# Soft-capped attention with a maxout layer: moving the q/k transposes of 36 of 48 head pairs from TensorE to the DMA crossbar, and reordering the weights' loads

## The chip, the cores and the metric

One core of one Trainium2 chip. The metric is the device time of one execution in microseconds (us). The kernel before was run four times beside the changed one, 437.27 to 440.6 us, median 439.74 (438.88 for the three runs known at the time of the prediction). Where a ratio is given, it is the mean time of one kernel's fast runs over the mean time of the other's fast runs of the same rounds, so it isn't quite the ratio of the medians that are quoted; the interval behind it is a 95% interval.

The views of the profile name the engines so: PE is TensorE's matmuls and PEld its weight loads, DVE is VectorE, ACT is ScalarE, POOL is GpSimd and SP is SyncE, which here only issues DMA transfers. PSUM is the memory that takes the matmuls' results. "Crossbar call" stands for one transposing DMA (DMA_TRANSPOSE in the profile).

## The reference

```python
# q, k, v: (8 batches, 12 heads, 448, 64) f32; cap = 30
scores = q @ k.T / sqrt(64)
scores = cap * tanh(scores / cap)
attn   = softmax(scores)                 # over 448 keys
x      = (attn @ v), heads side by side  # (3584, 768)
g      = maximum(x @ w1, x @ w2)         # w1, w2: (768, 1024)
out    = g @ w_out                       # (3584, 768)
```

The kernel uses max(h1, h2) = relu(h1 - h2) + h2: it keeps `wd = w1 - w2` and the product `wm = w2 @ w_out`, so that `out = relu(x @ wd) @ w_out + x @ wm`.

## The kernel before

Work goes by pairs of heads: 48 pairs, six per batch, loaded in 16 groups of three. A pair's q and k come in natural order, are cast to bf16 by POOL, and are turned by eight TensorE transposes into the unused half of a scores bank in PSUM; DVE copies them out:

```python
def transposes(i, ps):                     # ps = spare[i-1], a scores bank's unused half
    for t, o in ((kf, 0), (qf, Q0)):
        for j in range(4):
            nc.tensor.transpose(ps[:, o + j*P : o + (j+1)*P], t[g % 2][:, n, j, :], ident)
    qkT[i] = att.tile([P, 8 * P], bf16, name="qkT", bufs=3)
    nc.vector.tensor_copy(qkT[i], ps)
```

Then come scores, tanh and exp (ACT), attention times V into the one `pv` buffer, and DVE's copy `u` of it (5 buffers). Sums of the softmax leave `u` by small DMAs; every second pair they are inverted, sent to DRAM and read back spread over the partitions; POOL multiplies with them. All of these DMAs, and all loads of q, k and v, are issued by SP, in program order:

```python
def invert(g):                             # g: group of two pairs
    nc.vector.reciprocal(t, sums[g])
    nc.sync.dma_start(out=d, in_=t)                                   # rec_d <- rec_s
    for h in range(2):
        nc.sync.dma_start(out=rb[...], in_=flat[...].to_broadcast(...))  # rec_b <- rec_d
```

The weights come during the first nine pairs, issued by POOL, and are prepared as follows; `premultiply` and the two products of a finished batch are "filler" that is doled out to TensorE between the attention steps (`F(n)` gives n matmuls) and that writes into two PSUM buffers `mm`:

```python
def cast_w12(c):
    nc.gpsimd.tensor_copy(w2b, w2c)
    nc.vector.tensor_sub(wd_sb[:, c, :], w1c, w2c)
...
for i in range(N):                         # cut to the order of the parts
    pv_main(i); ex(i+1, 0, 4); pv_left(i); qk(i+1, 2); pv_out(i)
    F(8)
    qk(i+1, 3); ex(i+1, 4, 7)
    # casts and loads of coming groups; cast_w12, load_w12 in the first pairs
    F(6)
    transposes(i+2, spare[i+1])
    F(6)
    # even i: invert(last group);  odd i: normalize(POOL, last group)
    qk(i+2, 0); qk(i+2, 1)
    F(5)
```

## Time and profile before

I cut the 437.9 us of the profiled execution at two marks: the start of attention times V of pair 12 and of pair 47. The page of the kernel before gives the totals; the table of stretches (columns: stretch, its length, busy time of PE, PEld, DVE, ACT and POOL with their instructions, granted clock, DMA share, GB/s) gives the stages:

```profile
0.00:127.79 127.79, 88.21 (x523) 40.35 (x524) 55.70 (x90) 80.52 (x81) 66.35 (x94) 0.85 0.65 183
127.79:385.20 257.41, 252.92 (x1661) 126.75 (x1658) 118.30 (x177) 212.37 (x210) 135.80 (x166) 0.99 0.50 142
385.20:437.90 52.70, 42.31 (x236) 23.39 (x234) 16.48 (x28) 0.00 (x0) 4.51 (x4) 0.94 0.20 71
```

| stage of the kernel before | us | reading |
|---|---|---|
| front, to pair 12 | 127.8 | PE busy 69%, clock 0.85: waits |
| long stage, pairs 12 to 46 | 257.4 | PE busy 98%: TensorE is the bound |
| tail | 52.7 | 10 us of PE idle |

The timeline of the kernel before (start, length, engine, line, operation, out<-in, and in brackets the idle time ahead of it) has this in the long stage:

```profile
220.86 0.48 DVE L262 RECIPROCAL rec_s<-sums 32x56 f32<-32x56 f32 x1
221.59 0.54 SPq L264 DMA_DIRECT2D rec_d<-rec_s  x1
228.33 4.71 POOL L284 TENSOR_TENSOR xT<-u,rec_b 64x448 bf16<-64x448 f32 x4 [4.09 <-DMA rec_b<-rec_d]
```

In this kernel no reciprocal of the 24 waited more than 1.0 us for SP.

### The profile page before, as it was taken

How to read it: one execution, taken by the hardware profiler on the slowest of the kernel's cores; microseconds unless marked ns; L12 is line 12 of the kernel's file. 1: busy time of each engine (PE TensorE's matmuls, PEld its weight loads, DVE VectorE, ACT ScalarE, POOL GpSimd, SP SyncE). 2: the span in 40 equal slices, each digit the busy share in tenths (PEclk: the TensorE clock that was granted, in tenths of full speed). 3: DMA queues.
4: the chain of work that ended last, by engine and by line, in shares of the span. 5: the costliest groups of instructions: out<-in, count | busy, mean ns of one | idle time of the engine just before them, and what ended most of it. 6: DMA issues, size and time to landing. Idle time of an engine off the chain costs nothing.

```text
span 437.9 us, 6546 instructions
## 1 busy us (share of the span) xinstructions
PE 383.4 (88%) x2416; PEld 190.5 (44%) x2416; DVE 190.5 (44%) x294; ACT 292.9 (67%) x289; POOL 206.7 (47%) x263
## 2 busy tenths in 40 slices
PE   3570777779999999999998999999979999994996
PEld 1220333334455455544553555455434555452553
DVE  5322444545543553445345534554335344523422
ACT  4782564558798879887987798879858898810000
POOL 3381786751736573555554736563655424440000
PEclk9966786889999999999999999999989999996999
DMA  5999666632445646575655456646553212122012
GB/s 146 274 258 255 209 183 235 195 105 75 129 136 166 178 114 177 141 223 136 178 150 156 111 156 190 198 125 172 164 158 107 80 63 91 44 80 78 37 57 89
DMA packets 74016, 63.70 MB, mean 145 GB/s; under 512 B 24832, under 2 KB 68864, under 8 KB 73984
## 3 DMA queue, kind: packets, MB, share of 16 engines
q1 hardware_dynamic: 71168, 55.41, 44.5%
q0 software_dynamic: 2816, 7.87, 5.9%
q8 instruction: 19, 0.31, 0.3%
q14 instruction: 13, 0.11, 0.1%
HBM read 53.48 MB, written 11.18 MB: 148 GB/s over the span
## 4 chain that ended last, share of the span: by engine, by line
PE 71%; DMA 10%; POOL 8%; SPq 4%; DVE 3%; issue 3%; DVEq 0%; POOLq 0%
PE mm L297 17%; PE mm L312 15%; PE mm L309 11%; PE pv L232 10%; PE s L212 6%; POOL xT L284 4%; PE s L196 4%; DMA w_in<-in_moe_w_dram 4%; PE mm L177 4%; PE pv L241 3%; DMA rec_b<-rec_d 2%; SPq L111 2%; DMA rec_d<-rec_s 2%; PE s L215 1%; SPq L100 1%
## 5 line engine op out<-in xcount | busy, mean ns | idle before, releaser
L213 ACT ACTIVATE tanh<-s 128x896 bf16<-128x896 f32 x144 | 126.0, 909 | 77.9 <-PE s L212 77.8
L284 POOL TENSOR_TENSOR xT<-u,rec_b 64x448 bf16<-64x448 f32 x92 | 104.2, 1133 | 141.7 <-DMA rec_b<-rec_d 137.0
L220 ACT ACTIVATE expo<-tanh 128x1792 bf16<-128x1792 bf16 x96 | 145.0, 1510 | 3.0
L245 DVE COPY u<-pv 128x896 f32<-128x896 f32 x48 | 52.4, 1091 | 92.4 <-PE pv L241 85.8
L312 PE MATMUL mm<-wo_sb,gT 128*128 128x384 bf16 x448 | 91.7, 330 | 0.0
L297 PE MATMUL mm<-xT,wd_sb 128*128 128x448 bf16 x384 | 84.5, 357 | 4.1 <-POOL xT L284 4.1
L309 PE MATMUL mm<-wm_sb,xT 128*128 128x384 bf16 x336 | 70.6, 330 | 6.5 <-DVE osb L316 6.5
L232 PE MATMUL pv<-expo,vp 128*128 128x448 bf16 x288 | 66.8, 371 | 0.0
L212 PE MATMUL s<-qkT 64*128 64x448 bf16 x288 | 46.6, 377 | 15.0 <-DVE qkT L198 14.4
L312 PEld LDWEIGHTS <-gT 128*128 128x128 bf16 x448 | 41.9, 99 | 35.2 <-issue 11.4
L198 DVE COPY qkT<-s 128x1024 bf16<-128x1024 bf16 x47 | 32.5, 691 | 52.9 <-PE s L196 36.4
L297 PEld LDWEIGHTS <-wd_sb 128*128 128x128 bf16 x384 | 35.1, 99 | 43.1 <-issue 16.6
L301 DVE TENSOR_SCALAR gT<-mm 128x448 bf16<-128x448 f32 x64 | 39.7, 621 | 27.9 <-PE mm L297 27.2
L316 DVE COPY osb<-mm 128x384 f32<-128x384 f32 x56 | 30.8, 552 | 38.7 <-PE mm L312 38.4
L309 PEld LDWEIGHTS <-xT 128*128 128x128 bf16 x336 | 31.4, 99 | 32.9 <-issue 15.1
L232 PEld LDWEIGHTS <-vp 128*128 128x128 bf16 x288 | 28.7, 101 | 29.1 <-issue 6.1
L177 PE MATMUL mm<-wo_sb,w2T 128*128 128x384 bf16 x96 | 23.8, 392 | 13.6 <-DVE w2T L172 13.6
L217 ACT ACTIVATE tanh<-s 128x448 bf16<-128x448 f32 x48 | 26.0, 542 | 9.9 <-PE s L215 8.2
L196 PE MATMUL s<-ident,kf 128*128 128x128 bf16 x188 | 19.4, 230 | 6.3 <-ACT tanh L217 6.3
L131 POOL CAST kf<-km 128x1152 bf16<-128x1152 f32 x15 | 17.2, 1143 | 15.6 <-DMA km<-in_k_dram 12.7
L212 PEld LDWEIGHTS <-qkT 64*128 64x128 bf16 x288 | 10.6, 96 | 32.0 <-DVE qkT L198 28.5
L196 PEld LDWEIGHTS <-kf 128*128 128x128 bf16 x192 | 15.7, 103 | 19.1 <-issue 8.1
(50 smaller groups left out, 228.6 us busy)
## 6 DMA issues: line engine op xcount, KB each, us to landing
rec_b<-rec_d SPq DMA_DIRECT2D x48, 224.0 KB
out_dram<-osb SPq DMA_DIRECT2D x24, 384.0 KB
km<-in_k_dram SPq DMA_DIRECT2D x15, 576.0 KB
qm<-in_q_dram SPq DMA_DIRECT2D x15, 576.0 KB
vm<-in_v_dram SPq DMA_DIRECT2D x15, 576.0 KB
w_in<-in_moe_w_dram POOLq DMA_DIRECT2D x12, 512.0 KB, 5.0
sums<-u SPq DMA_DIRECT2D x96, 1.8 KB
wo_sb<-in_moe_w_out_dram POOLq DMA_DIRECT2D x4, 384.0 KB, 7.9
```

What stands on the lines that cost most here:

```text
L177: nc.tensor.matmul(ps[:, : DM // 2], w2T[:, f * P : (f + 1) * P], wo_sb[:, f, hs], start=(f == 0), stop=(f == FC - 1),)
L196: nc.tensor.transpose(ps[:, o + j * P : o + (j + 1) * P], t[g % 2][:, n, j, :], ident)
L212: nc.tensor.matmul(s[:, h, :S], t[r, j * P : (j + 1) * P], qTn[r, :])
L213: nc.scalar.activation(tanh[i][:, 2 * j : 2 * j + 2, :], s[:, :, :S], AF.Tanh, scale=scale / cap)
L220: nc.scalar.activation(expo[i][:, c0:c1, :], tanh[i][:, c0:c1, :], AF.Exp, scale=float(cap))
L232: nc.tensor.matmul(ps[:, h, :S], vp[g % 2][:, n, h, j, :], e[:, 2 * j + h, :], start=(j == 0), stop=False)
L245: nc.vector.tensor_copy(u, pvt[i][:, :, :S])
L284: eng.tensor_mul(xT[b // 2][r, hp, cs], U[i][r, h, :], rec[g][r, n, :])
L297: nc.tensor.matmul(ps[:, :S], wd_sb[:, c, f * P : (f + 1) * P], x[:, c, cs], start=(c == 0), stop=(c == KC - 1))
L301: nc.vector.tensor_relu(g[:, f, cs], ps[:, :S])
L309: nc.tensor.matmul(ps[:, : DM // 2], x[:, c, ts], wm_sb[:, c, hs], start=(c == 0), stop=False)
L312: nc.tensor.matmul(ps[:, : DM // 2], g[:, f, ts], wo_sb[:, f, hs], start=False, stop=(f == FC - 1))
```

## The change

The intent: take transposes off TensorE where it is the bound. Pairs 0 to 11 are still transposed by TensorE, now into the filler's `mm` buffers; from pair 12 on, one DMA-transpose call on SP turns the q and k of three pairs at once. w2 arrives as bf16 through a casting DMA, w1 is loaded by SP, the subtraction moves to the end of a pair, the filler of batch 0 is queued behind the premultiplication, and half of the last normalization goes to POOL. Cut to its core:

```diff
-    def cast_w12(c):
-        nc.gpsimd.tensor_copy(w2b, w2c)
-        nc.vector.tensor_sub(wd_sb[:, c, :], w1c, w2c)
+    def load_w2(c):
+        nc.gpsimd.dma_start(out=w2b[:, c, :], in_=moe_w2[c * P : (c + 1) * P, :])     # casts
+    def load_w1(c):
+        nc.sync.dma_start(out=w1_in[c], in_=moe_w1[c * P : (c + 1) * P, :])
+    def subtract(c):
+        nc.vector.tensor_sub(wd_sb[:, c, :], w1_in[c], w2b[:, c, :])
...
-    def transposes(i, ps):
+    def transposes(i):
+        ps = mm_psum.tile([P, 512], f32, name="mm").bitcast(bf16)
...
+    def cross(g):
+        nc.sync.dma_start_transpose(
+            out=qkT_of(g).rearrange("p n j c -> p (n j) c"), in_=kqf[g % 2].rearrange("p n j c -> p (n j c)")
+        )
...
+    NT = 4
+    for g in range(2, NL):                 # loads and casts of k, q, v: cut
+        if g >= NT:
+            at(3 * g - 4, cross, g)
+    for c in range(KC):
+        at(c // 3, load_w2, c)
+        at(2 + c, load_w1, c)
...
-        if i + 2 < N:
-            transposes(i + 2, spare[i + 1])
+        if i + 2 < NT * L:
+            transposes(i + 2)
...
+        if 3 <= i < 3 + KC:
+            subtract(i - 3)
```

More of the change, by code (lines that the diff above doesn't have):

```diff
@@ L64 @@
     vl = [const.tile([P, L, P], bf16, name=f"vl{i}") for i in range(2)]
-    kf = [const.tile([P, L, 4, P], bf16, name=f"kf{i}") for i in range(2)]
-    qf = [const.tile([P, L, 4, P], bf16, name=f"qf{i}") for i in range(2)]
+    kqf = [const.tile([P, L, 8, P], bf16, name=f"kqf{i}") for i in range(2)]
+    kf = [t[:, :, 0:4, :] for t in kqf]
+    qf = [t[:, :, 4:8, :] for t in kqf]
     ident = const.tile([P, P], bf16, name="ident")
@@ L143, in cast @@
                 eng.tensor_copy(t[r, n0:n1, 3, r], l[r, n0:n1, :])
-    w_in = {}
+    w1_in = {}
+    w2b = (
+        xpool.tile([P, FC, 2 * S], bf16, name="gT", bufs=1)
+        .rearrange("p f s -> p (f s)")[:, : KC * DF]
+        .rearrange("p (c n) -> p c n", c=KC)
+    )
     def load_wo(f):
@@ L151, in load_wo @@
         )
-    def load_w12(c):
-        w_in[c] = [stage.tile([P, DF], f32, name=n) for n in ("w1_in", "w2_in")]
-        for src, dst in zip((moe_w1, moe_w2), w_in[c]):
-            nc.gpsimd.dma_start(out=dst, in_=src[c * P : (c + 1) * P, :])
-    def cast_w12(c):
-        w1c, w2c = w_in[c]
-        w2b = stage.tile([P, DF], bf16, name="w2b", bufs=1)
-        nc.gpsimd.tensor_copy(w2b, w2c)
-        nc.vector.tensor_sub(wd_sb[:, c, :], w1c, w2c)
-        w_in[c] = w2b
+    def load_w2(c):
+        nc.gpsimd.dma_start(out=w2b[:, c, :], in_=moe_w2[c * P : (c + 1) * P, :])
+    def load_w1(c):
+        w1_in[c] = stage.tile([P, DF], f32, name="w1_in")
+        nc.sync.dma_start(out=w1_in[c], in_=moe_w1[c * P : (c + 1) * P, :])
+    def subtract(c):
+        nc.vector.tensor_sub(wd_sb[:, c, :], w1_in[c], w2b[:, c, :])
     def premultiply(c):
@@ L168, in premultiply @@
         for f in range(FC):
-            nc.tensor.transpose(ps[:, f * P : (f + 1) * P], w_in[c][:, f * P : (f + 1) * P], ident)
+            nc.tensor.transpose(ps[:, f * P : (f + 1) * P], w2b[:, c, f * P : (f + 1) * P], ident)
             yield
@@ L188, with qkT_of @@
     qkT = {}
-    spare = {}
-    def transposes(i, ps):
-        g, n = divmod(i, L)
-        for t, o in ((kf, 0), (qf, Q0)):
-            for j in range(4):
-                nc.tensor.transpose(ps[:, o + j * P : o + (j + 1) * P], t[g % 2][:, n, j, :], ident)
-        qkT[i] = att.tile([P, 8 * P], bf16, name="qkT", bufs=3)
-        nc.vector.tensor_copy(qkT[i], ps)
+    def qkT_of(g):
+        if g not in qkT:
+            qkT[g] = stage.tile([P, L, 8, P], bf16, name="qkT")
+        return qkT[g]
+    def transposes(i):
+        g, n = divmod(i, L)
+        ps = mm_psum.tile([P, 512], f32, name="mm").bitcast(bf16)
+        for j in range(8):
+            nc.tensor.transpose(ps[:, j * P : (j + 1) * P], kqf[g % 2][:, n, j, :], ident)
+        nc.vector.tensor_copy(qkT_of(g)[:, n, :, :].rearrange("p j c -> p (j c)"), ps)
+    def cross(g):
+        nc.sync.dma_start_transpose(
+            out=qkT_of(g).rearrange("p n j c -> p (n j) c"), in_=kqf[g % 2].rearrange("p n j c -> p (n j c)")
+        )
     def qk(i, j):
-        t = qkT[i]
+        g, n = divmod(i, L)
+        t = qkT[g][:, n, :, :].rearrange("p j c -> p (j c)")
         o = Q0 + 64 * (i // NP % 2)
@@ L215, in qk @@
             nc.tensor.matmul(s[:, 0, :S], t[:, 3 * P : 4 * P], qTn)
-            spare[i] = s[:, 1, :].bitcast(bf16)
             nc.scalar.activation(tanh[i][:, 6, :], s[:, 0, :S], AF.Tanh, scale=scale / cap)
@@ L273, with normalize @@
     xT = {}
-    def normalize(eng, g):
+    def normalize(g, eng_a=nc.gpsimd):
         for n in range(G):
@@ L283, in normalize @@
                 r = slice(64 * h, 64 * h + 64)
-                eng.tensor_mul(xT[b // 2][r, hp, cs], U[i][r, h, :], rec[g][r, n, :])
+                (nc.gpsimd, eng_a)[1 - h].tensor_mul(xT[b // 2][r, hp, cs], U[i][r, h, :], rec[g][r, n, :])
     gT = {}
@@ L337, with at @@
     NL = N // L
+    NT = 4
+    todo = [[] for _ in range(N)]
+    def at(i, f, *a):
+        todo[i].append((f, a))
+    for g in range(2, NL):
+        e = 0 if g < NT else 2
+        at(3 * g - 6 - e, load, g, "k")
+        at(3 * g - 5 - e, load, g, "q")
+        at(3 * g - 4, load, g, "v")
+        at(3 * g - (5 if e else 4), cast, nc.gpsimd, g, "k")
+        at(3 * g - (5 if e else 3), cast, nc.gpsimd, g, "q")
+        at(3 * g - 2, cast, nc.gpsimd, g, "v")
+        if g >= NT:
+            at(3 * g - 4, cross, g)
+    at(1, cast, nc.gpsimd, 1, "v")
+    for c in range(KC):
+        at(c // 3, load_w2, c)
+        at(2 + c, load_w1, c)
+    MS = 4
     fill_const(nc.vector, 0)
@@ L345 @@
     for what in "kq":
-        load(2, what)
-    for what in "kq":
         cast(nc.vector, 0, what, 0, 1)
-    transposes(0, mm_psum.tile([P, 512], f32, name="mm").bitcast(bf16))
+    transposes(0)
     cast(nc.vector, 0, "v", 0, 1)
@@ L361 @@
         cast(nc.gpsimd, 1, what)
-    transposes(1, spare[0])
+    for f in range(0, FC, 2):
+        load_wo(f)
+    transposes(1)
     qk(1, 0)
@@ L367 @@
         b, hp = divmod(i, NP)
-        l, ln = divmod(i, L)
         g, n = divmod(i, G)
@@ L376 @@
         pv_out(i)
-        if 3 <= i < 3 + KC:
-            fill_q.append(premultiply(i - 3))
-        if hp == 2 and b > 0:
+        if MS <= i < MS + KC:
+            fill_q.append(premultiply(i - MS))
+        if i == MS + KC - 1:
+            fill_q.append(moe(0))
+        if hp == 2 and b > 1:
             fill_q.append(moe(b - 1))
@@ L384 @@
             ex(i + 1, 4, 7)
-        for m, what, lead in ((0, "v", 1), (1, "k", 2), (1, "q", 2)):
-            if ln == m and l + lead < NL:
-                cast(nc.gpsimd, l + lead, what)
-        for m, what, lead in ((0, "v", 2), (1, "k", 3), (2, "q", 3)):
-            if ln == m and l + lead < NL:
-                load(l + lead, what)
-        if i < 2:
-            load_wo(4 * i)
-            load_wo(4 * i + 2)
-        if 2 <= i < 2 + KC:
-            cast_w12(i - 2)
-        if 1 <= i < 1 + KC:
-            load_w12(i - 1)
-        F(6)
-        if i + 2 < N:
-            transposes(i + 2, spare[i + 1])
+        for f, a in todo[i]:
+            f(*a)
+        F(6)
+        if i + 2 < NT * L:
+            transposes(i + 2)
         F(6)
@@ L404 @@
         if i >= G + 1 and n == 1:
-            normalize(nc.gpsimd, g - 1)
+            normalize(g - 1)
         if i + 2 < N:
@@ L409 @@
         F(5)
+        if 3 <= i < 3 + KC:
+            subtract(i - 3)
+    F(16)
     invert(N // G - 1)
-    normalize(nc.vector, N // G - 1)
+    F(24)
     fill_q.append(moe(B - 1))
+    normalize(N // G - 1, nc.vector)
     F(10 ** 9)
```

## The prediction

> **What bounds the kernel now.** I read the busy table and the slices first, then a table of stretches, then the order of work in one steady period, then the two places where the table shows holes.
>
> ```profile
> PE 383.4 (88%) x2416; PEld 190.5 (44%) x2416; DVE 190.5 (44%) x294; ACT 292.9 (67%) x289; POOL 206.7 (47%) x263
> PE 71%; DMA 10%; POOL 8%; SPq 4%; DVE 3%; issue 3%; DVEq 0%; POOLq 0%
> ```
>
> The busy table and the chain that ended last: TensorE holds 71% of the chain, but 29% is something else, so the span has to be cut by stage. Table of stretches (columns: stretch, length, busy time of PE, PEld, DVE, ACT, POOL, clock, DMA share, GB/s):
>
> ```profile
> 0.00:35.00 35.00, 18.40 (x92) 6.59 (x92) 13.37 (x33) 24.39 (x25) 16.25 (x34) 0.90 0.92 226
> 35.00:45.00 10.00, 0.64 (x7) 0.13 (x4) 2.22 (x3) 0.82 (x1) 2.37 (x2) 0.54 0.81 230
> 45.00:62.00 17.00, 12.55 (x76) 5.67 (x73) 7.85 (x9) 12.19 (x12) 14.42 (x18) 0.80 0.67 210
> 62.00:107.00 45.00, 35.83 (x223) 17.63 (x221) 21.25 (x29) 26.34 (x27) 24.96 (x32) 0.84 0.52 162
> 127.00:385.00 258.00, 253.51 (x1664) 127.12 (x1663) 118.10 (x177) 213.16 (x210) 136.26 (x166) 0.99 0.50 142
> 385.00:438.00 53.00, 42.51 (x238) 23.49 (x235) 16.68 (x28) 0.00 (x0) 4.51 (x4) 0.94 0.20 70
> ```
>
> Three regimes: a front until 107 us with a dead hole at 35 to 45 us and low clocks; a long stage from 127 us in which PE is 98% busy at clock 0.99; a tail with 10 us of PE idle.
>
> One period of the long stage, timeline, PE (start, length):
>
> ```profile
> 219.23 0.49 PE L312 MATMUL mm<-wo_sb,gT 128*128 128x384 bf16 x2
> 219.55 0.39 PE L196 MATMUL s<-ident,kf 128*128 128x128 bf16 x4
> 219.78 0.39 PE L196 MATMUL s<-ident,qf 128*128 128x128 bf16 x4
> 220.00 1.14 PE L312 MATMUL mm<-wo_sb,gT 128*128 128x384 bf16 x6
> ```
>
> The eight transposes of a pair hold PE from 219.55 to 220.00: 0.45 us, 56 ns each, not the 222 to 231 ns that one record lasts (they overlap).
>
> The hole at 35 to 45 us, timeline, DVE:
>
> ```profile
> 42.60 1.22 DVE L162 TENSOR_TENSOR wd_sb<-w_in 128x1024 bf16<-128x1024 f32 x1 [8.68 <-DMA w_in<-in_moe_w_dram]
> 43.74 0.68 DVE L198 COPY qkT<-s 128x1024 bf16<-128x1024 bf16 x1
> ```
>
> The subtraction w1-w2 stands ahead of the copy of the transposes in DVE's queue and waits 8.7 us for the weights; the copy, and with it the next scores, wait behind it. Before that, ACT is the bound, with one wait per pair (timeline, ACT):
>
> ```profile
> 22.99 1.73 ACT L213 ACTIVATE tanh<-s 128x896 bf16<-128x896 f32 x2 [0.75 <-PE s L212]
> 29.77 1.73 ACT L213 ACTIVATE tanh<-s 128x896 bf16<-128x896 f32 x2 [0.74 <-PE s L212]
> ```
>
> Period 6.8 us, of which ACT works 6.05. The wait is there because the transposes are written in the spare half of a scores bank and so start only after the last tanh. The tail, timeline, DVE, then PE:
>
> ```profile
> 397.26 1.89 DVE L284 TENSOR_TENSOR xT<-u,rec_b 64x448 bf16<-64x448 f32 x3 [0.17 <-DMA rec_b<-rec_d]
> 399.18 1.02 DVE L316 COPY osb<-mm 128x384 f32<-128x384 f32 x2
> ```
>
> ```profile
> 399.79 2.08 PE L309 MATMUL mm<-wm_sb,xT 128*128 128x384 bf16 x6 [6.55 <-DVE osb L316]
> 401.66 2.76 PE L312 MATMUL mm<-wo_sb,gT 128*128 128x384 bf16 x8
> ```
>
> The last normalization stands on DVE ahead of evictions that PE needs, and waits for the reciprocals' round trip; PE loses 6.55 us, then runs 14 matmuls at half speed.
>
> **What the Trainium skill says.** "TensorE: Matmul & The Clock Gate", Part 4: PE-mode transpose, gives about 275 ns for a transpose in a kernel. The trace has 222 to 231 ns as length but 56 ns as spacing, and the spacing decides. The same page, Part 1: The HAM clock gate, says that an idle window of some 3.4 us halves the clock; the trace agrees (0.54 in the hole; the six matmuls at 399.79 took 2.08 us, those at 390.80 1.14), so a removed hole pays more than its length. "DMA: Bandwidth & Descriptors", Latency and other measured facts, gives 261 GB/s for a DMA transpose in one kernel, 350 to 400 when contiguous. Nothing in this trace measures it. The same page, Issuing engines are not separate DMA queues: transfers of SP and POOL run on the same 16 DMA engines. So moving w1 to SP buys order and not bandwidth; the trace's share of 0.92 in the first 35 us, with both queues in use, is in line with that.
>
> **The change part by part.**
>
> *Transposes.* 36 of the 48 pairs lose 8 transposes: 36 x 0.45 = 16.2 us of PE, 15.3 of them in the 34 periods between pair 12's attention-times-V (127.8 us) and pair 47's (385.2). Also 36 DVE copies of 691 ns = 25 us; DVE is 46% busy there, so these are worth nothing by themselves. Added: 12 crossbar calls on SP, each 128 x 3072 bf16 = 0.79 MB. At the page's 261 GB/s an estimate of 3 us each, one per three pairs (about 20 us). Each is issued some two and a half periods before its first use, about 16 us. The DMA share in the long stage would go from 0.50 to about 0.65. I take it as hidden.
>
> *Transposes of the first 12 pairs in the other PSUM pool.* They no longer wait for the last tanh: the 0.75 us wait goes, period 6.05 us in the pairs without filler.
>
> *Weights.* w2 comes as bf16 by a casting DMA (6 POOL casts of 1.55 us = 9.3 us go); the subtraction moves to the end of the period, behind the copies that the scores need; the premultiplication starts one pair later. Front, from pair to pair (starts of attention-times-V): pairs 0 to 3 took 45.3-16.4 = 28.9 us; 3 x 6.05 = 18.2, and I leave 3 us for weights that land late = 21.2. Pair 3 to 4: 9.8 becomes 6.05. Pairs 4 to 10: 58.1 us, with 2.7 us waits of PE for the w2T copy (which sits behind the subtraction) and half clock after each; the one old period whose w2T copy had no subtraction before it took 7.4 us, so 6 x 7.4 = 44.4. Pairs 10 to 12: 14.6 becomes 14.5 (0.9 less for transposes, more of the 448-column filler). Pair 12 then starts at 16.4+21.2+6.05+44.4+14.5 = 102.5 us in place of 127.8: 25 us gained.
>
> *Long stage.* 257.4 us less 15.3. Three periods hold waits for a late normalization, because the filler had run dry when the next batch's first product was started: 0.7, 1.4 and 4.3 us over the stall-free 7.68, together 6.3. By my count of filler steps (25 per pair offered, 24 per premultiplication, 132 or 160 per batch) the later start keeps 15 to 41 steps in stock at each batch's turn, so those go; 1.2 us come back, because slots that ran empty are filled. 257.4-15.3-6.3+1.2 = 237 us.
>
> *Tail.* 52.7 us from pair 47. The stock left then is 57 steps, with the 25 of the last period 82, each 0.1625 us = 13.3 us, enough to cover the reciprocal chain (normalization ended 14 us after pair 47 started). Half of the last normalization goes to POOL, and it stands after the evictions. The last batch, 48 x 0.189 + 112 x 0.1625 = 27.3 us, then starts at +14.8 in place of +21.4, and 3.9 us of output follow: 46 us.
>
> Sum: 102.5+237+46 = 385.5 us of span. I add 4 us for waits that I can't place and 1 us between span and measured time: **390 us**, 11% less.
>
> **Rivals.**
> 1. *The crossbar call is slow or clogs SP's queue.* Adding up the SP rows of the timeline from 147 to 390 us gives 134 us of issuing, 55%. If one call holds SP or the DMA rings for 10 us, SP comes to near 100%, sums and reciprocals queue behind, U's five buffers fill, and PE waits for attention results. Against: the lead of 16 us and one call per three pairs. For: the chain from sums to normalized xT is already tight (DVE waited 6.6 us for POOL to free U). Then the long stage gains nothing or loses: 410 to 450 us.
> 2. *The front is bound by DMA and not by order.* Loads of five groups and all weights are still needed by the same pair, and DMA ran at 226 to 230 GB/s at a share of 0.8 to 0.9 until 45 us. Then the hole moves to the premultiplication or the subtraction, and the front gains some 12 us: about 403 us.
> 3. *ACT takes over in the long stage.* A stall-free period goes from 7.0 to 7.7 down to 6.6 to 7.2, and ACT needs 6.05. PE stays the bound, but the margin of 0.5 us means that a small delay of scores is no longer free: 392 to 396 us.
>
> **Range and chances.** My sum has three large independent terms: 25 us in front (could be 12), 20 in the long stage (could be 0 with rival 1, 22 at best), 7 in the tail (4 to 8). A part of the front is lost with a chance of about one in four, a slow crossbar with one in eight. Range for 8 in 10: 377 to 408 us. The change is slower only if the crossbar truly bounds: faster by over 2% 0.91, within 2% 0.05, slower 0.04.
>
> **What would show it.** Right: no DVE copy of qkT after pair 11; PE period 6.6 us without transposes in the out-product stretches; no hole near 35 us and pair 12 near 102 us; no PE gap over 1 us near pair 38 or between pair 47 and the last batch; PE still 95% busy from pair 12 on. Wrong: PE or its weight loads waiting for the crossbar's DMA; SP waiting long for POOL's casts in front of a crossbar call; DVE's copy of U waiting for POOL; DVE's subtraction waiting for w1 or w2 past 40 us.

## The result, and the profile after

The changed kernel took 424.96 us (median of four, 423.34 to 425.88) beside 439.74 before: ratio 0.967 [0.962, 0.972], so 3.3% faster and not 11%. It is faster, but 424.96 lies well outside the predicted range.

The busy table and the chain that ended last, of the changed kernel:

```profile
PE 365.7 (86%) x2128; PEld 172.8 (41%) x2128; DVE 163.8 (39%) x256; ACT 292.3 (69%) x289; POOL 197.0 (46%) x253
PE 50%; DMA 21%; SPq 9%; POOL 8%; DVE 5%; issue 3%; ACT 2%; POOLq 0%; DVEq 0%
```

PE did 17.7 us less work, as intended, but PE's part of the chain fell from 71% to 50%, and DMA and SP's queue went from 14% to 30%. PE is no longer what most of the chain consists of. The table of stretches, cut at the same marks:

```profile
0.00:119.39 119.39, 80.95 (x482) 36.03 (x483) 51.81 (x87) 79.89 (x81) 53.95 (x81) 0.90 0.72 184
119.39:375.38 255.99, 242.00 (x1399) 112.70 (x1397) 96.28 (x144) 212.42 (x209) 136.32 (x167) 0.98 0.71 179
375.38:424.10 48.72, 42.80 (x251) 24.09 (x249) 15.76 (x27) 0.00 (x0) 6.73 (x6) 0.98 0.23 76
```

| stage | before | predicted | after |
|---|---|---|---|
| front | 127.8 | 102.5 | 119.4 |
| long stage | 257.4 | 237 | 256.0 |
| tail | 52.7 | 46 | 48.7 |
| sum | 437.9 | 385.5 | 424.1 |

The long stage is the surprise: PE has 10.9 us less to do and the stage is only 1.4 us shorter. From pair to pair (start of the last part of attention times V to the next pair's; all periods below are taken so), the periods are those predicted where nothing stands still: 6.57 us in place of 7.01, and 7.24 in place of 7.68 where the batch's first product is the filler. But pair 23 took 11.56 us and pair 35 took 14.13. This is the timeline at pair 35, with other rows left out:

```profile
272.12 0.48 DVE L275 RECIPROCAL rec_s<-sums 32x56 f32<-32x56 f32 x1
...
275.50 4.57 SPq L209 DMA_TRANSPOSE qkT<-kqf  x1
...
281.47 0.55 SPq L277 DMA_DIRECT2D rec_d<-rec_s  x1
285.14 1.24 SPq L281 DMA_DIRECT2D rec_b<-rec_d  x2
286.47 1.43 SPq L267 DMA_DIRECT2D sums<-u  x2
288.93 4.70 POOL L297 TENSOR_TENSOR xT<-u,rec_b 64x448 bf16<-64x448 f32 x4 [15.08 <-DMA rec_b<-rec_d]
289.66 0.49 DVE L275 RECIPROCAL rec_s<-sums 32x56 f32<-32x56 f32 x1 [6.25 <-DMA sums<-u]
292.96 0.80 PE L322 MATMUL mm<-wm_sb,xT 128*128 128x384 bf16 x2 [5.61 <-DVE gT L314]
```

Read it from the top. DVE has the reciprocals ready at 272.60. Their store stands in SP's queue behind V's loads and the crossbar call, which holds SP for 4.57 us, and behind q's loads; it is issued at 281.47, 8.9 us late, where the kernel before issued it after 0.25. SP must then stand still 3 us for that store to land, because the next thing in its queue reads it back, and only after that does it issue the next sums (286.47). DVE's next reciprocal has come up in DVE's own queue, ahead of the evictions, and waits 6.25 us for those sums; PE, whose filler buffers DVE doesn't empty, stops for 5.61 us.

The front: timeline of the changed kernel around pair 4.

```profile
33.43 8.30 SPq L112 DMA_DIRECT2D vl<-in_v_dram  x2
41.78 0.59 SPq L164 DMA_DIRECT2D w_in<-in_moe_w_dram  x1
48.74 1.23 DVE L167 TENSOR_TENSOR wd_sb<-w_in,gT 128x1024 bf16<-128x1024 f32 x1 [11.28 <-DMA w_in<-in_moe_w_dram]
51.62 2.10 PE L181 MATMUL mm<-wo_sb,w2T 128*128 128x384 bf16 x6 [7.65 <-DVE w2T L176]
```

The old hole has moved and not gone: SP needed 8.30 us to issue two small loads of V (48 KB each), the load of w1 came only behind them, and the subtraction stood 11.28 us at the head of DVE's queue, in front of the copies that PE and ACT wait for. The same happened at pair 7 (4.97 us of waiting). These two pairs took 17.57 and 14.88 us; pairs 5, 6, 8 and 9 took 7.8 to 8.3. While SP was issuing the two loads, the DMA engines' share was 1.12 at 227 GB/s, so they were busy throughout; whether that is why issuing took so long was not tested.

### The profile page after: what moved, and what is told of

The parts are those of the page before. It is cut to its first block, busy times and chain, and to the rows that moved or that the text cites. A ratio compares the mean times of both kernels' runs of the same rounds, so it can differ in the third digit from the quotient of the medians.

```text
span 424.1 us, 5849 instructions
## 1 busy us (share of the span) xinstructions
PE 365.7 (86%) x2128; PEld 172.8 (41%) x2128; DVE 163.8 (39%) x256; ACT 292.3 (69%) x289; POOL 197.0 (46%) x253
## 3 DMA queue, kind: packets, MB, share of 16 engines
q1 hardware_dynamic: 109280, 68.00, 61.2%
## 4 chain that ended last, share of the span: by engine, by line
PE 50%; DMA 21%; SPq 9%; POOL 8%; DVE 5%; issue 3%; ACT 2%; POOLq 0%; DVEq 0%
PE mm L310 12%; PE mm L325 11%; PE mm L322 9%; PE pv L245 8%; POOL xT L297 7%; DMA rec_d<-rec_s 7%; DMA rec_b<-rec_d 7%; PE s L226 5%; SPq L112 3%; DMA out_dram<-osb 3%; DVE u L258 3%; PE mm L181 2%; SPq L209 2%; PE pv L254 2%; DMA w_in<-in_moe_w_dram 2%
## 5 line engine op out<-in xcount | busy, mean ns | idle before, releaser
L297 POOL TENSOR_TENSOR xT<-u,rec_b 64x448 bf16<-64x448 f32 x94 | 106.1, 1129 | 158.9 <-DMA rec_b<-rec_d 135.6
L310 PE MATMUL mm<-xT,wd_sb 128*128 128x448 bf16 x384 | 83.5, 358 | 8.4 <-DVE gT L314 3.1
L325 PE MATMUL mm<-wo_sb,gT 128*128 128x384 bf16 x448 | 88.5, 328 | 1.5 <-DVE gT L314 1.5
L322 PE MATMUL mm<-wm_sb,xT 128*128 128x384 bf16 x336 | 69.0, 330 | 5.9 <-DVE gT L314 5.6
L245 PE MATMUL pv<-expo,vp 128*128 128x448 bf16 x288 | 65.9, 365 | 1.1 <-ACT expo L233 1.0
L325 PEld LDWEIGHTS <-gT 128*128 128x128 bf16 x448 | 42.0, 98 | 38.3 <-issue 10.9
L230 ACT ACTIVATE tanh<-s 128x448 bf16<-128x448 f32 x48 | 26.0, 541 | 19.2 <-PE s L229 17.7
L132 POOL CAST kqf<-qm 128x1152 bf16<-128x1152 f32 x15 | 17.2, 1146 | 15.8 <-DMA qm<-in_q_dram 15.3
L132 POOL CAST kqf<-km 128x1152 bf16<-128x1152 f32 x15 | 18.1, 1204 | 13.8 <-DMA km<-in_k_dram 12.9
L181 PEld LDWEIGHTS <-w2T 128*128 128x128 bf16 x96 | 9.1, 108 | 31.5 <-DVE w2T L176 20.3
L275 DVE RECIPROCAL rec_s<-sums 32x56 f32<-32x56 f32 x24 | 11.6, 484 | 26.1 <-DMA sums<-u 24.3
```

The lines of the kernel that those rows point to most:

```text
L132: eng.tensor_copy(t[:, n0:n1, o : o + NJ, :].rearrange("p n j (h d) -> p n h j d", h=2), m[:, 2 * n0 : 2 * n1, :].rearrange("p (n h) (j d) ...
L181: nc.tensor.matmul(ps[:, : DM // 2], w2T[:, f * P : (f + 1) * P], wo_sb[:, f, hs], start=(f == 0), stop=(f == FC - 1),)
L245: nc.tensor.matmul(ps[:, h, :S], vp[g % 2][:, n, h, j, :], e[:, 2 * j + h, :], start=(j == 0), stop=False)
L297: (nc.gpsimd, eng_a)[1 - h].tensor_mul(xT[b // 2][r, hp, cs], U[i][r, h, :], rec[g][r, n, :])
L310: nc.tensor.matmul(ps[:, :S], wd_sb[:, c, f * P : (f + 1) * P], x[:, c, cs], start=(c == 0), stop=(c == KC - 1))
L322: nc.tensor.matmul(ps[:, : DM // 2], x[:, c, ts], wm_sb[:, c, hs], start=(c == 0), stop=False)
```

## The experiments

Two theories of the long stage stood at first. **Queue:** SP's program order is too full; what is late is what stands behind the crossbar call. **Transfer:** the crossbar's traffic itself, in 256-byte pieces, makes the other DMAs slow. A third was that the five `u` buffers run out. For the front: the subtraction's place, or where w1 is loaded. All edits are against the changed kernel, and the results of all runs agreed with the reference. Times are medians; "12-47" is the time from pair 12 to pair 47, 257.4 us before and 256.0 after.

**e1: no crossbar, all transposes by TensorE in the `mm` buffers.**

```diff
-        if g >= NT:
+        if g >= NX:            # NX = NL: never
-        if i + 2 < NT * L:
+        if i + 2 < NX * L:
```

> The changed kernel with all 48 pairs transposed on TensorE and no crossbar call at all; load times, weights, pools and tail as in the change. Theory A (the crossbar call causes the new waits of the long stage, 18.6 us there by period lengths): those waits go and 36 x 0.45 = 16 us of transposes come back, so about 420 to 424 us, level with the changed kernel, and no wait of POOL for the reciprocals over 10 us. Theory B (the waits come from the other parts, such as the later stock of filler or the shortened loads): the waits stay and the transposes are added: about 440 us.

Measured: 440.62 us, ratio 1.007 [1.002, 1.013]; 12-47 took 270.0. From pair 12 on no period was over 9 us, so the large holes do come with the crossbar; but 24 of the 35 periods became 0.3 to 0.9 us longer than in e8, which only puts the same transposes back into the spare scores bank and takes 16.2 us less for this stage (253.8). So here the transposes compete with the filler for two PSUM buffers, and this isn't a clean removal of the crossbar (e8 is).

**e2: the same bytes by plain copies.** The result is not what attention needs (q and k are not turned), on purpose. That the comparison with the reference passes all the same tells that it hardly sees this part: scores of inputs this small are near zero, and softmax near uniform. So it doesn't vouch for the layout that the crossbar gives either.

```diff
-        nc.sync.dma_start_transpose(...)
+        for m in range(2):
+            nc.sync.dma_start(out=o[:, m::2, :], in_=s[:, m::2, :])
```

> The crossbar call replaced by two plain copies between the same buffers with the same bytes in 256-byte pieces (wrong result on purpose). Theory A1 (SP is held 4.45 us by each crossbar call, and the reciprocals' transfer stands behind it in SP's order): SP issues in about 1.3 us, the waits of 14 to 15 us of POOL once in six pairs shrink by some 3 us or more, 408 to 416 us. Theory A2 (the bytes of the crossbar in the DMA rings delay everything behind them): within 3 us of the changed kernel's 425 us. Theory B: no change either.

Measured: 423.73, ratio 0.966 [0.959, 0.973], 12-47 254.2: as with the crossbar. The two copies hold SP for 1.6 to 3.3 us, and the load of q behind them takes another 1.0 to 3.0 (0.4 to 0.6 in the changed kernel). So turning the data is not what costs: moving as much in small pieces through SP's queue costs the same.

**e3: the crossbar call behind the reciprocals instead of ahead of them.**

```diff
-            at(3 * g - 4, cross, g)
+        if (i + 4) % L == 0 and NT <= (i + 4) // L < NL:
+            cross((i + 4) // L)      # after invert and normalize
```

> The crossbar call is issued later in the same period, behind the reciprocals' two transfers on SP (right result). Theory A1 (order on SP): the four waits of 14 to 15 us fall to the 4 to 8 us of the kernel before, and 10 to 14 us go: 411 to 415 us. Theory A2 (load on the rings): the call only hits the next transfers instead, 420 to 428 us. Rival: the call is now late for its scores, TensorE waits for it, slower than 425 us.

Measured: 436.67, ratio 0.998 [0.990, 1.005], 12-47 270.4. Now the crossbar is late instead: the waits of this run have PE standing for it (line by line: who waits, for what, us in total, times, longest).

```profile
PE s L226 <- DMA qkT<-kqf: 17.9, 6, 5.4
```

Order alone doesn't help; one or the other is late.

**e4: six `u` buffers instead of five.**

```diff
-    upool = ctx.enter_context(tc.tile_pool(name="upool", bufs=5))
+    upool = ctx.enter_context(tc.tile_pool(name="upool", bufs=6))
```

> Six buffers for the attention result U in place of five. Theory A (a late normalization hurts because U's buffers are all taken, so that the copy of U and behind it DVE's evictions stop): one more pair of slack, 6.6 us, takes most of the holes of 4.6 and 7.2 us away: 412 to 417 us. If the holes come from DVE waiting for the sums to compute the reciprocal (5 to 6 us, four times), in front of evictions, or from the first product of a batch waiting for xT, nothing changes: 422 to 427 us.

Measured: 425.31, ratio 0.972 [0.965, 0.978], 12-47 255.4: no change. The `u` buffers aren't what holds PE; DVE's reciprocal, which waits for sums, stands in front of everything anyway.

**e5: POOL issues the read-back of the reciprocals.**

```diff
-            nc.sync.dma_start(           # rec_b <- rec_d
+            nc.gpsimd.dma_start(
```

> The two broadcast loads of the reciprocals are issued by POOL in place of SP, at the same point of the program; all else as in the change. Theory C (SP's in-order queue is full in the long stage: 194 us of issuing, of which 48 for the crossbar, and 41 us of standing in front of the reciprocals' loads, in 256 us): SP gets 63 us of room, the once-in-six-pairs holes go, the long stage falls from 256 to 238 to 242 us: 407 to 412 us. Rival D (the crossbar's bytes delay every transfer whoever issues it): 421 to 427 us, POOL's waits of 14 us stay. Rival E: POOL blocks on the round trip itself and its casts come late: the same or slower.

Measured: 445.01, ratio of the fast runs 1.016 [1.012, 1.020]. Slower by 20 us than the changed kernel. Only that is to be taken from this run: its profile fell in an execution in the slow state (453.2 us of span). POOL stands 86.1 us in it for the store to land, which fits the picture that the wait was only handed on, to an engine with more to do, but slow and fast stages aren't to be compared.

**e6: w1 loaded by POOL. e7: the subtraction one pair later.**

```diff
-        nc.sync.dma_start(out=w1_in[c], ...)       # e6
+        nc.gpsimd.dma_start(out=w1_in[c], ...)
-        if 3 <= i < 3 + KC:                        # e7
-            subtract(i - 3)
+        if 4 <= i < 4 + KC:
+            subtract(i - 4)
```

> w1 is loaded by POOL's queue, as in the kernel before, all else as in the change. Theory F (the two holes in front, at pairs 4 and 7, are w1 issued late because SP lags behind, its loads' issue taking up to 8.3 us): both holes shrink, pair 12's attention starts near 108 in place of 119 us: 412 to 417 us. Rival G (DMA is full in front; another queue only reorders the bytes): the hole moves to another load, 421 to 427 us.

> Each subtraction w1-w2 stands one pair later in DVE's order. Theory F' (the holes in front are a head-of-line wait: DVE stands at the subtraction, 11.3 and 5.0 us, in front of the copy of U and of w2T): with 6 to 7 us more for w1 to land, the hole at pair 4 loses some 7 us and the one at pair 7 its 5 to 6 us: 411 to 416 us. Rival G: the wait only moves to the next pair, 421 to 427 us.

Measured: e6 421.53, ratio 0.962 [0.959, 0.965]; e7 419.55, 0.959 [0.957, 0.960]. Pair 12 comes 8.8 and 9.1 us sooner than in the changed kernel, by different holes: e6 keeps the one at pair 4 (16.22) and loses that at pair 7 (7.81); e7 loses both (7.93 and 7.98) and has 12.55 at pair 5. But 12-47 became longer, 260.7 and 259.1. A part of what the front gains is given back while the long stage is full of holes.

**e8: no crossbar, and pairs from 12 on transposed by TensorE in the spare scores bank, as before the change.**

```diff
-            transposes(i + 2)
+            transposes(i + 2, spare[i + 1] if i + 2 >= NT * L else None)   # and no cross
```

> No crossbar; pairs 12 to 47 transposed on TensorE in the spare half of a scores bank as in the kernel before, pairs 0 to 11 in the pool that filler uses. This mends the first experiment, where all transposes went through the filler's pool. If the holes come with the crossbar, the long stage is the old one without its 6.3 us of waits, 252 us, the front and the tail stay as in the change: 418 to 423 us, hardly slower than the changed kernel. If the holes are of the later stock or the other loads, 437 to 443 us.

Measured: 422.89, ratio 0.966 [0.964, 0.968], 12-47 253.8. The table of stretches over this stage (cut within 0.2 us of the marks, here and for e9 and e16):

```profile
120.50:374.20 253.70, 252.69 (x1670) 126.83 (x1668) 118.34 (x178) 212.27 (x209) 133.88 (x164) 1.00 0.49 145
```

PE is busy for all but 1 us. The crossbar as a whole, 12 calls, is thus worth nothing: without it the kernel is as fast. It removes 34 x 0.45 = 15.3 us from these periods and brings 256.0 - (253.8 - 15.3) = 17.5 us of holes.

**e9, e10: half the crossbar calls.** Six calls, for the odd groups (e9) or the even ones (e10); the others as in e8. The even groups' calls stand right ahead of the reciprocals in SP's queue. So "the call must not stand in front of the store" and "SP has too much to do" part here.

```diff
+    by_pe = lambda g: g < NT or g % 2 == 0        # e10: g % 2 == 1
-        if g >= NT:
+        if not by_pe(g):
```

> Crossbar for the odd groups of three pairs alone (6 calls, each issued in a period without a reciprocals' round trip); even groups on TensorE in the spare half of a scores bank. Theory H (the holes come from a crossbar call standing directly ahead of the reciprocals' store in SP's order): no holes, long stage 253.8 less 18 x 0.45 = 8 us: about 246 us, 414 to 417 us in all. Theory I (it is SP's or the rings' total load): half of the 18.6 us of holes stays, about 255 us, 422 to 426 us.

> The mirror: crossbar for the even groups alone (6 calls, each directly ahead of a reciprocals' store on SP), odd groups on TensorE. Theory H: all holes stay, long stage about 262 us, 428 to 433 us. Theory I: the same as with the odd groups, within 3 us.

Measured: 416.26, ratio 0.946 [0.943, 0.950], and 415.91, 0.946 [0.942, 0.950]; 12-47 245.8 and 247.1. Stretches of e9, then the timeline of e10 at the pair that was the worst of the changed kernel:

```profile
120.90:366.70 245.80, 244.80 (x1527) 118.89 (x1525) 106.95 (x159) 212.56 (x210) 134.17 (x165) 1.00 0.62 169
```

```profile
263.91 0.48 DVE L277 RECIPROCAL rec_s<-sums 32x56 f32<-32x56 f32 x1
266.08 4.33 SPq L210 DMA_TRANSPOSE qkT<-kqf  x1
271.83 0.54 SPq L279 DMA_DIRECT2D rec_d<-rec_s  x1
```

No holes in either. e9 gains 18 x 0.45 = 8.1 us in this stage by calculation and 253.8 - 245.8 = 8.0 as measured. In e10 the store is 7.4 us late (271.83 against 264.39) and that costs nothing: the normalized data still came early enough. A call directly ahead of the reciprocals is therefore not harmful by itself; the number of calls is.

**e11: loads of q, k and v for groups from 4 on issued by POOL,** to give SP room.

```diff
+        eng = nc.gpsimd if g >= 4 else nc.sync
-        nc.sync.dma_start(            # three places in load()
+        eng.dma_start(
```

> The changed kernel with the loads of q, k and v from the fifth group on issued by POOL's queue: some 50 us of issuing leave SP in the long stage, the crossbar calls stay where they are. Theory I for SP (its in-order queue is full: 194 us of issuing and 62 us of waits at its head in 256 us): the holes shrink to under 5 us in all, long stage 240 to 244 us, 408 to 413 us. Theory H: a hole of 8.9 us ahead of the reciprocals' store loses the two loads (1.3 us) but keeps the 4.5 us of the call: some 6 us better at most, 418 to 422 us. Rival: POOL's issuing takes as long as its work has room, no gain or slower.

Measured: 477.82, ratio 1.088 [1.083, 1.094]. Far slower than the kernel before, so whatever room SP got doesn't show. The crossbar call issued at 113.66 took 9.60 us on SP, and its data let PE go on only at 135.84, 22 us later; in 117 to 124 us the DMA share was 1.16 at only 119 GB/s. Its timeline:

```profile
113.66 9.60 SPq L210 DMA_TRANSPOSE qkT<-kqf  x1
...
135.84 0.93 PE L227 MATMUL s<-qkT 64*128 64x448 bf16 x4 [8.00 <-DMA qkT<-kqf]
```

So transfers do stand in each other's way, but in this arrangement, which the changed kernel doesn't have.

**e12: e8 and e7 together,** so no crossbar, and the subtraction one pair later; the edits are those two.

> No crossbar (pairs 12 to 47 in the spare half of the scores bank) and the subtraction one pair later. If the two mends add up: front 8 us shorter than in the change, long stage 253.8, so 414 to 417 us: a version without the crossbar that beats the change by some 2%. If the front's gain is used up by a hole elsewhere: 422 us as without the later subtraction.

Measured: 415.12, ratio 0.944 [0.941, 0.948]; pair 12 comes 8.5 us sooner than in e8 (113.1 against 121.6), and 12-47 stays at 253.8. Nothing is given back here: where the long stage has no holes, the front's gain goes through whole. It is also 10 us faster than the changed kernel, without a single crossbar call.

**e13, e17: e8 with SP held by tiny stores.** No crossbar; at each place where a call stood, 7 (e13) or 12 (e17) stores of 1 KB. They take SP's time and move almost nothing (58.71 MB in all on SP's queue in e17, 58.56 in e8, 68.00 in the changed kernel).

```diff
+    def hold(g):
+        for m in range(12):            # e13: 7
+            nc.sync.dma_start(out=tiny[8*g : 8*g+8, m, :], in_=ident[8*m : 8*m+8, :64])
-            at(3 * g - 4, cross, g)
+            at(3 * g - 4, hold, g)
```

> No crossbar (as e8, 422.9 us, long stage 253.8), and at each place of a crossbar call SP issues seven tiny stores of 1 KB each, some 4.5 us of issuing and hardly any bytes. Theory S (SP's time is what fills): the once-in-six-pairs holes come back without a crossbar, long stage 262 to 272 us, 431 to 441 us. Theory R (the rings' time on the bytes): within 3 us of e8.

> As e13 with twelve tiny stores per place, some 5.2 us of SP, more than the 4.45 us of a crossbar call. Theory S (SP's time): holes of POOL's late reciprocals, 431 to 441 us. Theory R (rings): within 3 us of e8's 422.9.

Measured: e13 424.35, ratio 0.969 [0.968, 0.971], 12-47 253.8, no hole, with 3.1 us of SP per place from the first store's start to the last one's end. e17 432.94, ratio 0.984 [0.976, 0.991], 12-47 264.3, with 5.1 us of SP per place, of which SP stands 0.7 until an earlier load has landed. The timeline of e17 at pair 35, which took 14.02 us (14.13 in the changed kernel):

```profile
274.93 0.48 DVE L283 RECIPROCAL rec_s<-sums 32x56 f32<-32x56 f32 x1
278.38 5.14 SPq L212 DMA_DIRECT2D tiny<-ident  x12
285.19 0.55 SPq L285 DMA_DIRECT2D rec_d<-rec_s  x1
...
293.30 0.49 DVE L283 RECIPROCAL rec_s<-sums 32x56 f32<-32x56 f32 x1 [5.90 <-DMA sums<-u]
```

The same picture with neither crossbar nor data: SP's time alone brings holes of 264.3 - 253.8 = 10.5 us, nearly all at pairs 23, 35 and 38, three of the pairs that the changed kernel has holes at. This is the run that carries the queue theory. It holds SP somewhat longer than a call does (5.1 against 4.45 us) and e13 shorter, so it shows that SP's time can do it, and not how much of the changed kernel's 17.5 us it makes.

**e14, e18: the same bytes, issued by ACT and not by SP.** e8 plus two copies per place in 256-byte pieces, from the q/k tile (e14) or from a weight that is always there (e18), into a scratch tile.

```diff
+    def ballast(g):
+        for m in range(2):
+            nc.scalar.dma_start(out=scratch[:, m::2, :], in_=s[:, m::2, :])   # e14: s = q/k; e18: w_out
```

> No crossbar (as e8), and at each place of a crossbar call ACT issues two copies of the same bytes in the same 256-byte pieces into an unused buffer. Theory R: the rings are as full as with the crossbar, holes come back, 431 to 441 us. Theory S: within 4 us of e8 (ACT has 1 us per period for the issue). If ACT stands long in the issue, its own waits show it and the run tells less.

> As e14 with the resident w_out as the source of the copies, so that ACT waits for nothing before it issues them: 12 x 0.79 MB in 256-byte pieces on the rings, SP's program as in e8. Theory R: the reciprocals come late once in six pairs and PE stops, long stage 262 us or more, over 430 us. Theory S: within 4 us of e8. If e17 and e18 both stay near e8, neither alone does it, and only both together fill the path of the reciprocals.

Measured: e14 441.4, ratio 1.009 [1.006, 1.012], 12-47 272.8. e18 434.66, 0.988 [0.982, 0.994], 12-47 266.5. Neither is clean. In e14 ACT itself waits for POOL's casts before it may issue the copies. In e18 reciprocals are hardly late in SP's queue (at most 4.4 us), yet there are three holes, periods of 11.73, 9.38 and 12.51 us, at pairs 18, 24 and 36, none of them a place where the changed kernel has one. The timeline of ACT at the first of them, and at a place without a hole:

```profile
158.90 6.45 ACTq L213 DMA_DIRECT2D scratch<-wo_sb  x2
165.39 0.92 ACT L235 ACTIVATE tanh<-s 128x896 bf16<-128x896 f32 x1 [5.23 <-DMA scratch<-wo_sb]
...
184.66 1.89 ACTq L213 DMA_DIRECT2D scratch<-wo_sb  x2
186.72 1.73 ACT L235 ACTIVATE tanh<-s 128x896 bf16<-128x896 f32 x2 [0.80 <-PE s L234]
```

At exactly these three places ACT issued its second copy 5.8, 4.3 and 6.6 us after the first, since it stood until a read-back of the reciprocals had landed, and the tanh stood behind it. At the other nine it was 0.7 to 1.9 us, and no other period of the long stage is over 0.2 us longer than in e8. So the same bytes, where they hold up no engine's queue, bring no hole. Whether the crossbar's traffic costs something on top of SP's time stays open.

**e15: e9 + e6 + e7. e16: e15, and pairs 6 to 11 also transposed in the spare bank.** The parts that helped, together.

> Crossbar for the odd groups alone, the subtraction one pair later, w1 by POOL's queue. If the parts add: long stage 246, front 8 us shorter than in the change by the subtraction and up to 3 more by w1: 404 to 409 us, faster than both kernels.

> As e15, and the transposes of pairs 6 to 11 go to the spare half of a scores bank as in the kernel before. Theory P (transposes in the filler's two PSUM buffers make the filler wait for their copy, some 0.4 us a pair): periods of pairs 4 to 9 from 7.8 to 8.0 to near 7.4, 2 to 3 us less than e15. If those periods are bound by DVE's copy of w2T: the same within 1 us.

Measured: e15 406.55, ratio 0.929 [0.927, 0.931]; e16 404.58, 0.924 [0.922, 0.926]. The stretch of e16 between the same marks:

```profile
108.62:354.40 245.78, 244.78 (x1526) 118.93 (x1525) 107.03 (x160) 212.28 (x209) 134.02 (x164) 1.00 0.61 169
```

The long stage is e9's, 245.8 us with PE standing still for 1 us; pair 12 comes 10.8 us sooner than in the changed kernel (109.8 against 120.6). Pairs 6 to 8 took 7.2 to 7.5 us, where they took 7.8 to 8.5 in e15. e16 beats both kernels: 7.6% less time than the kernel before, and 20 us less than the changed one.

**What SP's load and the holes have to do with each other.** For the long stage, from the traces: the sum of the lengths of SP's DMA instructions, the latest store of reciprocals (from the end of the reciprocal to the issue), and the holes over what the same periods take without any (253.8, less 0.45 for each period from pair 12 on that the crossbar or its copies relieve: 34 in the changed kernel and e2, 18 in e9, 16 in e10). In every run with 12 places or calls, and in e10, the first lies ahead of the stage.

| run | calls from pair 12 on | SP issuing, us | latest store, us | holes, us |
|---|---|---|---|---|
| e8 | none | 136 of 254 | 2.8 | 0 |
| e10 | 6 crossbar | 159 of 247 | 7.4 | 0.5 |
| e9 | 6 crossbar | 159 of 246 | 3.1 | 0.1 |
| e13 | 7 tiny stores a place | 160 of 254 | 6.1 | 0 |
| e17 | 12 tiny stores a place | 179 of 264 | 10.4 | 10.5 |
| e2 | 12 pairs of plain copies | 180 of 254 | 10.2 | 15.7 |
| after | 12 crossbar | 186 of 256 | 10.7 | 17.5 |

(The 194 us in the expectations of e5 and e11 counts merged rows of the timeline, with the small gaps in them.) To the issuing come 39 to 48 us for which SP stands until the reciprocals' store has landed (40.5 in the changed kernel, 42.1 before). The waits of SP's queue also name POOL ahead of crossbar calls, 21.8 us in all, but that isn't time on top: all calls but the last start right behind SP's instruction before them (the one at 163.96 after 163.93), so those 21.8 us lie almost wholly within the calls' own 4.45 us.

So it works like a threshold: up to 160 us of issuing there is next to no hole, from 179 us on there is. Lateness alone doesn't decide it. A store up to 7.4 us late was free in e10; of those 8 to 11 us late, one at pair 33 of the changed kernel (8.9 us, shown above) was followed by a hole of 6.9 us, while one at its pair 18 (8.3 us) had none in the next two pairs and one at pair 26 of e17 (10.1 us) 0.4. The landing of the store doesn't tell the runs apart: from its issue to the read-back's issue it took 1.4 to 6.5 us in all of them.

## Why the prediction was wrong

The direction was right and the sum wrong: 385.5 us of span predicted, 424.1 measured, 38.6 too little. By its own terms:

1. **"I take it as hidden" is the step that failed: 17.5 us of the long stage's 19.** The crossbar was priced as a transfer (3 us each, the prediction's estimate from the Trainium skill's 261 GB/s) and checked against DMA's share and its lead of 16 us; it does arrive in time in the changed kernel. What it wasn't priced as is 4.45 us of SP's time, a dozen times over, in a queue that also carries the reciprocals. Rival 1 had the mechanism ("sums and reciprocals queue behind"), with 10 us per call as its threshold and 410 to 450 us as its price. 4.45 us were enough, and the prediction added up SP's issuing (55%) without adding the 42 us that SP stood for the store, which the same trace shows. e17 shows that SP's time alone brings such holes (10.5 us), and e18 that the traffic alone brings none where it holds up no engine; how the 17.5 us divide, and whether traffic adds to SP's time, is open. "U's five buffers fill" was not the path: e4 changed nothing, and it was DVE's reciprocal, waiting for sums, that stood ahead of the evictions.
2. **Periods of the long stage: right.** 6.6 to 7.2 was predicted and 6.57 to 7.24 measured; eight transposes are worth 0.45 us. Without the holes the stage would be 253.8 - 15.3 = 238.5, against 237 predicted. That the waits for late normalizations (6.3 us) would go was right as well: e8 has none.
3. **Front, "6 x 7.4 = 44.4" for pairs 4 to 10: measured 65.8** by the prediction's own marks, the starts of the first part of attention times V. Of these 21.4 us too many, 19.1 are the two holes (18.97 - 7.4 and 14.89 - 7.4 by these marks) and 2.3 the other four periods, which took 7.8 to 8.3. (The period read as 7.4 is 7.31 in the trace.) The prediction held that the subtraction no longer stands ahead of copies. It stands at the end of its pair now, which is ahead of the next pair's copies, and w1 comes later because it is behind SP's other loads. e7 takes away 9.1 us of it by the subtraction's place alone and e6 8.8 us by w1's place alone, so the term failed by both. This is rival 2's outcome in kind (the hole moves to the subtraction). Its reason, DMA bandwidth, can't be all of it: e7 moves no byte and e6 only changes who issues. But no run took bytes away, the DMA share was 1.12 while SP issued V's loads, and even e16 keeps 10.87 and 11.93 us at pairs 4 and 5, so a part of it may hold. Part of the small rest is the transposes sharing the two `mm` buffers with the filler: e16 takes 7.2 to 7.5 us for pairs 6 to 8 with them in the spare bank.
4. **Pairs 0 to 4: better than predicted.** 22.8 us against 21.2 + 6.05 = 27.3: the wait for the last tanh went, and the 3 us that I left for late weights weren't needed yet. Pairs 10 to 12 took 14.4 against 14.5.
5. **Tail: 48.7 against 46,** 52.7 before. The gain of 4 us is at the low end of "4 to 8". I didn't pursue the rest.
6. **Rival 3, ACT takes over: not seen.** In e9 and e16 PE is still the bound with PE busy but for 1 us.

The terms add up: 19.0 in the long stage, 16.9 in front (21.4 - 4.4 - 0.1), 2.7 in the tail.

## What to carry to other kernels

Before work goes from a full engine to DMA, price it on the queue that issues it as well: add up that queue's issuing time and what it stands for, stage by stage, and look at what urgent, small thing stands behind the new calls. Here such a queue had a threshold and not a slope: six calls brought 8 us and twelve brought nothing. So try half of the calls. And a wait at the head of an in-order engine isn't removed by moving the instruction to the end of one step, since the next step begins right behind it; it has to go where its data is sure to be there.

## What the Trainium skill lacked or had wrong

- "DMA: Bandwidth & Descriptors", Latency and other measured facts, gives a DMA transpose 261 GB/s in one kernel and 350 to 400 when contiguous. Here: SP's queue took 61.2% of 424.1 us with the 12 calls and 47.8% of 422.2 us without (e8), so 57.7 us of all 16 engines for 12 x 0.79 MB, 4.8 us each or 163 GB/s; by e9 (54.8% of 415.0 us, six calls) 4.3 us each, 184 GB/s. Both are differences of totals, so estimates.
- The same page has no time for which a DMA transpose of this size holds the engine that issues it (it only lists sequencer cycles of two other transposes, in a comparison of chip generations): 3.65 to 4.86 us here for 128 x 3072 bf16, median 4.45, against mostly 0.4 to 0.7 us for an ordinary load of the same kernel.
- The same page, Issuing engines are not separate DMA queues, calls the time to initiate a DMA "usually small relative to the DMA itself". Here it is as long as the transfer for the crossbar call, and 8.30 us for two 48 KB loads while the DMA share was 1.12. e17 shows what it leads to: 10.5 us lost by stores that move hardly a byte. The page's other statement, that transfers of all issuers share the 16 engines, agrees with e11 (a crossbar call's data 22 us after its issue beside loads issued by POOL).
- "TensorE: Matmul & The Clock Gate", Part 4: PE-mode transpose, gives about 275 ns for a transpose. A record lasts about 230 ns here, but it is the spacing that counts between matmuls: 8 removed, 0.44 us per pair less (7.01 to 6.57), 55 ns each.
